# A scalar broadcast to 128 partitions by DMA at the head of the sync queue, with the first x load moved to the ACT queue

One core of a Trainium2 chip. The metric is the device time of one execution in microseconds (us).

## The reference

```python
def setup_inputs():
    B, S, D = 512, 32, 640
    # x, fx: (B, S, D) bfloat16; alpha: (1,) bfloat16

def reference(x, fx, alpha):
    return x + alpha * fx
```

Two tensors of 20.97 MB are read and one is written: 62.92 MB in all, and one multiply-add for each element.

## The kernel before

Each tensor is seen as 128 partitions by 81920 columns and cut into five chunks of 16384 columns (4.19 MB, 32 KB a partition). VectorE computes `f * alpha + x` on a chunk in place. It needs alpha as a column, one value a partition. The kernel before loads alpha as a single element and spreads it with a matmul against a row of ones.

```python
def alpha_to_lanes(nc, consts, psum, alpha, eng):
    P = nc.NUM_PARTITIONS
    a_1 = consts.tile([1, 1], alpha.dtype, name="a_1")
    eng.dma_start(out=a_1[:], in_=alpha[None, :])
    ones = consts.tile([1, P], alpha.dtype, name="ones")
    nc.vector.memset(ones[:], 1.0)
    a_ps = psum.tile([P, 1], F32, name="a_ps")
    nc.tensor.matmul(a_ps[:], ones[:], a_1[:], start=True, stop=True)
    a_f = consts.tile([P, 1], F32, name="a_f")
    nc.vector.tensor_copy(out=a_f[:], in_=a_ps[:])
    return a_f
# ... (pools: xs has 4 buffers, fs has 2)
    a_f = alpha_to_lanes(nc, consts, psum, alpha, nc.scalar)

    def load_x(k):
        xt[k] = xs.tile([P, CHUNK], x.dtype, tag="x", name="x_t")
        nc.sync.dma_start(out=xt[k][:], in_=xv[:, bass.ts(k, CHUNK)])

    def load_f(k):
        ft[k] = fs.tile([P, CHUNK], fx.dtype, tag="f", name="f_t")
        nc.sync.dma_start(out=ft[k][:], in_=fxv[:, bass.ts(k, CHUNK)])
# ...
    load_x(0)
    load_f(0)
    load_x(1)
    load_f(1)
    load_x(2)
    compute(0)
    load_f(2)
    store(0)
    load_x(3)
    compute(1)
# ... (goes on in this way; the last chunk is computed and stored in two halves)
```

All large transfers, stores too, go through the sync queue in this order. In the profile each issuing queue appears as a ring (q1 belongs to SyncE, here "sync" or SP; q10 to ScalarE, "ACT"). A ring's transfers are carried out by 16 DMA engines, and each is recorded as packets, here one for each partition's row.

Of the kernel before, what the change touches and what calls it, by code (L numbers as in the profile page):

```python
# [1 line left out]

# [4 lines left out]

ACT = mybir.ActivationFunctionType
ALU = mybir.AluOpType
F32 = mybir.dt.float32  # L10
BF16 = mybir.dt.bfloat16

CHUNK = 16384


def alpha_to_lanes(nc, consts, psum, alpha, eng):

    P = nc.NUM_PARTITIONS
    a_1 = consts.tile([1, 1], alpha.dtype, name="a_1")
    eng.dma_start(out=a_1[:], in_=alpha[None, :])  # L20
    ones = consts.tile([1, P], alpha.dtype, name="ones")
    nc.vector.memset(ones[:], 1.0)  # L22
    a_ps = psum.tile([P, 1], F32, name="a_ps")
    nc.tensor.matmul(a_ps[:], ones[:], a_1[:], start=True, stop=True)  # L24
    a_f = consts.tile([P, 1], F32, name="a_f")
    nc.vector.tensor_copy(out=a_f[:], in_=a_ps[:])  # L26
    return a_f


@with_exitstack  # L30
def kernel(
    ctx: ExitStack,
    tc: tile.TileContext,
    x: bass.AP,
    fx: bass.AP,
    alpha: bass.AP,
    out: bass.AP,
):
    nc = tc.nc
    P = nc.NUM_PARTITIONS  # L40
    xv = x.flatten_outer_dims().rearrange("(p n) d -> p (n d)", p=P)
    fxv = fx.flatten_outer_dims().rearrange("(p n) d -> p (n d)", p=P)
    ov = out.flatten_outer_dims().rearrange("(p n) d -> p (n d)", p=P)
    F = xv.shape[1]
    K = F // CHUNK
    assert K * CHUNK == F and K == 5

    consts = ctx.enter_context(tc.tile_pool(name="consts", bufs=1))
    psum = ctx.enter_context(tc.tile_pool(name="psum", bufs=1, space=bass.MemoryType.PSUM))
    xs = ctx.enter_context(tc.tile_pool(name="xs", bufs=4))  # L50
    fs = ctx.enter_context(tc.tile_pool(name="fs", bufs=2))
    ctx.enter_context(tc.manual_schedule())

    a_f = alpha_to_lanes(nc, consts, psum, alpha, nc.scalar)
    xt, ft = {}, {}

    def load_x(k):
        xt[k] = xs.tile([P, CHUNK], x.dtype, tag="x", name="x_t")
        nc.sync.dma_start(out=xt[k][:], in_=xv[:, bass.ts(k, CHUNK)])  # L59

    def load_f(k):
        ft[k] = fs.tile([P, CHUNK], fx.dtype, tag="f", name="f_t")
        nc.sync.dma_start(out=ft[k][:], in_=fxv[:, bass.ts(k, CHUNK)])

    def compute(k, parts=1):
        n = CHUNK // parts
        for j in range(parts):
            s = bass.ts(j, n)
            nc.vector.scalar_tensor_tensor(  # L69
                out=xt[k][:, s],  # L70
                in0=ft[k][:, s],
                scalar=a_f[:],
                in1=xt[k][:, s],
                op0=ALU.mult,
                op1=ALU.add,
            )

    def store(k, j=0, parts=1):
        n = CHUNK // parts
        nc.sync.dma_start(  # L80
            out=ov[:, k * CHUNK + j * n : k * CHUNK + (j + 1) * n],
            in_=xt[k][:, bass.ts(j, n)],
# [12 lines that stand above are left out]
    load_f(3)  # L95
    store(1)
    load_x(4)
    compute(2)
    load_f(4)
    store(2)  # L100
    compute(3)
    store(3)
    compute(4, 2)
    store(4, 0, 2)
    store(4, 1, 2)


# [1 line left out]
_INS = ['x', 'fx', 'alpha']  # L109
_OUTS = [((512, 32, 640), 'bfloat16')]  # L110


# [23 lines left out]
```

## Time and profile before

| | before |
|---|---|
| time, median of 3 | 152.79 us (152.72 to 152.88) |
| span of the profiled run | 150.6 us |
| sync queue's share of 16 DMA engines | 98.0% |
| VectorE busy | 86.9 us (58%) |
| bytes moved, mean rate | 62.92 MB, 418 GB/s |

How to read it: a resource that is busy for 98% of the span bounds the kernel. Work on other engines then matters only if it makes that resource start later, pause or do more. The lines behind this are in the prediction.

### The profile page before, as it was taken

How to read it: one execution, taken by the hardware profiler on the slowest of the kernel's cores; microseconds unless marked ns; L12 is line 12 of the kernel's file. 1: busy time of each engine (PE TensorE's matmuls, PEld its weight loads, DVE VectorE, ACT ScalarE, POOL GpSimd, SP SyncE). 2: the span in 40 equal slices, each digit the busy share in tenths (PEclk: the TensorE clock that was granted, in tenths of full speed). 3: DMA queues.
4: the chain of work that ended last, by engine and by line, in shares of the span. 5: the costliest groups of instructions: out<-in, count | busy, mean ns of one | idle time of the engine just before them, and what ended most of it. 6: DMA issues, size and time to landing. Idle time of an engine off the chain costs nothing.

```text
span 150.6 us, 85 instructions
## 1 busy us (share of the span) xinstructions
PE 0.2 (0%) x1; PEld 0.1 (0%) x1; DVE 86.9 (58%) x8; POOL 0.2 (0%) x4
## 2 busy tenths in 40 slices
PE   0000000000000000000000000000000000000000
PEld 0000000000000000000000000000000000000000
DVE  0000009999679998499991006999900089997000
POOL 0000000000000000000000000000000000000000
DMA  6999999999999999799999999999999999999994
GB/s 200 444 453 435 418 418 418 418 444 453 444 453 435 418 418 418 339 444 470 418 418 418 418 418 435 435 435 453 426 435 444 418 418 435 435 435 405 426 444 205
DMA packets 2306, 62.92 MB, mean 418 GB/s; under 512 B 258, under 2 KB 258, under 8 KB 258
## 3 DMA queue, kind: packets, MB, share of 16 engines
q1 hardware_dynamic: 2304, 62.92, 98.0%
q10 hardware_dynamic: 2, 0.00, 0.0%
HBM read 41.94 MB, written 20.97 MB: 418 GB/s over the span
## 4 chain that ended last, share of the span: by engine, by line
DMA 56%; DVE 29%; DVEq 6%; issue 0%; SPq 0%
DMA f_t<-in_fx_dram 56%; DVE x_t L69 29%; DVEq L131 6%; SPq L59 0%; DVEq L69 0%
## 5 line engine op out<-in xcount | busy, mean ns | idle before, releaser
L69 DVE SCALAR_TENSOR_TENSOR x_t<-f_t,a_f,x_t 128x16384 bf16<-128x16384 bf16 (+1 forms) x6 | 86.6, 14439 | 49.5 <-DMA f_t<-in_fx_dram 49.5
L26 DVE COPY a_f<-a_ps 128x1 f32<-128x1 f32 x1 | 0.2, 159 | 1.1 <-PE a_ps L24 1.1
L22 DVE MEMSET ones<- 1x128 bf16 x1 | 0.2, 165 | 0.8 <-PEq L120 0.8
L24 PE MATMUL a_ps<-a,ones 1*128 1x1 bf16 x1 | 0.2, 159 | 1.9 <-DMA a<-in_alpha_dram 1.9
L120 POOL MEMSET const-bfloat16-1.0<- 128x1 bf16 x1 | 0.1, 102 | 0.0
L120 POOL MEMSET const-uint8-127<- 128x1 uint8 x1 | 0.1, 102 | 0.0
L24 PEld LDWEIGHTS <-ones 1*128 1x128 bf16 x1 | 0.1, 100 | 1.0 <-DVE ones L22 1.0
L120 POOL MEMSET const-float32-0.0<- 128x1 f32 x1 | 0.1, 99 | 0.2 <-issue 0.2
L120 POOL MEMSET const-float32-1.0<- 128x1 f32 x1 | 0.1, 99 | 0.0
## 6 DMA issues: line engine op xcount, KB each, us to landing
x_t<-in_x_dram SPq DMA_DIRECT2D x5, 4096.0 KB, 34.8
f_t<-in_fx_dram SPq DMA_DIRECT2D x5, 4096.0 KB, 32.1
out_dram<-x_t SPq DMA_DIRECT2D x4, 4096.0 KB, 36.5
out_dram<-x_t SPq DMA_DIRECT2D x2, 2048.0 KB, 15.2
a<-in_alpha_dram ACTq DMA_DIRECT2D x1, 0.0 KB
```

What stands on the lines that cost most here:

```text
L22: nc.vector.memset(ones[:], 1.0)
L24: nc.tensor.matmul(a_ps[:], ones[:], a_1[:], start=True, stop=True)
L26: nc.vector.tensor_copy(out=a_f[:], in_=a_ps[:])
L69: nc.vector.scalar_tensor_tensor(out=xt[k][:, s], in0=ft[k][:, s], scalar=a_f[:], in1=xt[k][:, s], op0=ALU.mult, op1=ALU.add,)
L120: nc = _bacc.Bacc("TRN2", target_bir_lowering=False, num_devices=1)
L131: with _tile.TileContext(nc) as tc:
```

## The change

Its intent: alpha comes as a finished column in one DMA, so that memset, matmul and PSUM (where the matmul's result goes) are not needed, and the first x load does not queue behind it, since it is issued from another engine at the same time.

```diff
-def alpha_to_lanes(nc, consts, psum, alpha, eng):
+def alpha_to_lanes(nc, consts, alpha, eng):
     P = nc.NUM_PARTITIONS
-    a_1 = consts.tile([1, 1], alpha.dtype, name="a_1")
-    eng.dma_start(out=a_1[:], in_=alpha[None, :])
-    ones = consts.tile([1, P], alpha.dtype, name="ones")
-    nc.vector.memset(ones[:], 1.0)
-    a_ps = psum.tile([P, 1], F32, name="a_ps")
-    nc.tensor.matmul(a_ps[:], ones[:], a_1[:], start=True, stop=True)
+    a_b = consts.tile([P, 1], alpha.dtype, name="a_b")
+    eng.dma_start(out=a_b[:], in_=alpha.to_broadcast((P, 1)))
     a_f = consts.tile([P, 1], F32, name="a_f")
-    nc.vector.tensor_copy(out=a_f[:], in_=a_ps[:])
+    nc.vector.tensor_copy(out=a_f[:], in_=a_b[:])
     return a_f
# ... (the PSUM pool goes)
-    a_f = alpha_to_lanes(nc, consts, psum, alpha, nc.scalar)
+    a_f = alpha_to_lanes(nc, consts, alpha, nc.sync)
     def load_x(k):
         xt[k] = xs.tile([P, CHUNK], x.dtype, tag="x", name="x_t")
-        nc.sync.dma_start(out=xt[k][:], in_=xv[:, bass.ts(k, CHUNK)])
+        eng = nc.scalar if k == 0 else nc.sync
+        eng.dma_start(out=xt[k][:], in_=xv[:, bass.ts(k, CHUNK)])
```

More of the change, by code (lines that the diff above doesn't have):

```diff
@@ L48 @@
     consts = ctx.enter_context(tc.tile_pool(name="consts", bufs=1))
-    psum = ctx.enter_context(tc.tile_pool(name="psum", bufs=1, space=bass.MemoryType.PSUM))
     xs = ctx.enter_context(tc.tile_pool(name="xs", bufs=4))
```

## The prediction

> **What bounds the kernel now.** I read the page's summary and its DMA queue part first, to see which resource is full. Then I read the table by stretches, to see whether it is full all the time, and last the timeline and the waits of the sync queue, to see who could let it run dry.
>
> The head of the page and the queue part:
>
> ```profile
> span 150.6 us, 85 instructions
> PE 0.2 (0%) x1; PEld 0.1 (0%) x1; DVE 86.9 (58%) x8; POOL 0.2 (0%) x4
> ...
> q1 hardware_dynamic: 2304, 62.92, 98.0%
> q10 hardware_dynamic: 2, 0.00, 0.0%
> HBM read 41.94 MB, written 20.97 MB: 418 GB/s over the span
> ```
>
> The sync queue's ring (q1) keeps all 16 DMA engines busy for 98.0% of the span. VectorE has 86.9 of 150.6 us. The ACT ring (q10) carries only alpha: one datum and one semaphore write, 2 packets. So this is a copy machine with an add beside it. Bytes over rate: the table by stretches gives the steady rate.
>
> ```profile
> 5.00:30.00 25.00, 0.00 (x0) 0.00 (x0) 7.16 (x1) 0.00 (x0) 1.00 1.00 431
> 30.00:60.00 30.00, 0.00 (x0) 0.00 (x0) 27.41 (x2) 0.00 (x0) 1.00 1.03 435
> 60.00:90.00 30.00, 0.00 (x0) 0.00 (x0) 17.28 (x1) 0.00 (x0) 1.00 0.99 422
> 90.00:120.00 30.00, 0.00 (x0) 0.00 (x0) 17.29 (x1) 0.00 (x0) 1.00 0.99 429
> ```
>
> The last two columns are the DMA share and GB/s. The share is 0.99 or more in every stretch, at about 431 GB/s. 62.92 MB at 431 GB/s is 146.0 us. The span has 4.6 us more: the same table cut finely shows no bytes before some point in 1.5 to 2.0 us and none after 149.0 (of 150.6), which is about 3.2 us; the remaining 1.4 us are the fill of the first packets and small dips. A change can therefore act on the time only through the moment at which the first bytes flow, the work or pauses added to the DMA engines, or a moment at which the queue runs empty.
>
> The chain of waits blames fx loads (56%) and VectorE (29%), which is how a transfer behind others in one FIFO looks: the f_t load "takes" 21.55 us from issue to landing because x_t's 4.19 MB stand before it (2 x 4.19 MB / 431 GB/s = 19.5 us, plus the start). I do not read that chain as a bound by VectorE: the DMA engines are full while VectorE runs.
>
> The start, from the timeline:
>
> ```profile
> 0.73 0.38 SPq L59 DMA_DIRECT2D x_t<-in_x_dram  x1
> 0.73 0.49 ACTq L20 DMA_DIRECT2D a<-in_alpha_dram  x1
> ...
> 1.16 0.43 SPq L63 DMA_DIRECT2D f_t<-in_fx_dram  x1
> ...
> 2.11 0.16 DVE L26 COPY a_f<-a_ps 128x1 f32<-128x1 f32 x1 [1.13 <-PE a_ps L24]
> ...
> 22.84 17.28 DVE L69 SCALAR_TENSOR_TENSOR x_t<-f_t,a_f,x_t 128x16384 bf16<-128x16384 bf16 x1 [20.57 <-DMA f_t<-in_fx_dram]
> ```
>
> SP and ACT issue their first DMAs at the same moment, 0.73 us. The alpha column is ready at 2.11 + 0.16 = 2.27 us, and its first reader starts at 22.84: the alpha path has 20.6 us of slack now.
>
> Can the queue run dry? The sync queue's own waits:
>
> ```profile
> SPq L80 <- DVE x_t L69: 55.5, 3, 28.7
> SPq L63 <- DVE x_t L69: 41.6, 3, 17.4
> ```
>
> Large, but harmless. Five loads are issued by 3.2 us, good for 5 x 4.19 MB / 431 = 48.7 us, that is till about 50; the sixth load is issued at 40.16 us, when the first multiply-add ends. There are 10 us in hand, and the later issues, counted the same way, have 6 us (the last half store) or more.
>
> **What the Trainium skill says.** (1) "DMA: Bandwidth & Descriptors", section "Issuing engines are not separate DMA queues": DMAs from sync, scalar and gpsimd run on the same 16 engines and interleave; several issuers save only sequencer time. The trace before fits: one ring alone already fills the engines to 98.0%. (2) The same page, "Queues, rings and completion order": an engine takes turns between the rings that have work, switching at packet boundaries. Nothing in the trace before shows it, as q10 carried only 2 packets; the changed kernel will. (3) The same page, "Bandwidth", the measured table: a 4 KB load to 128 partitions has a floor of about 0.67 us, read there as about 10.5 ns a packet. It is for DMAs issued from GpSimd, and no row of this trace has a load of 128 tiny elements. (4) The same page, "Specifications": below 512 B a transfer is not at line rate, because of a read-modify-write. The 258 packets under 512 B of the trace before, spread over the run, leave the share at 0.99 or more, so small packets as such are not dear here.
>
> **The change, part by part.**
>
> *Removed:* on VectorE one memset (0.165 us), on PE a weight load and a matmul (0.10 and 0.16 us), a PSUM tile, and two hand-overs between engines. All lie before 2.27 us with 20.6 us of slack. Worth 0 us. The copy to f32 (0.16 us) stays and now reads SBUF; it still lies ahead of the first multiply-add on VectorE, which waits anyway.
>
> *Moved: the first x load to ACT.* ACT issues at 0.73 us as SP did; its one issue took 0.49 us against 0.38, so the first bytes may come some 0.1 us later, or not at all later. Cost 0 to +0.1 us. The bytes are the same, and x and fx of the first chunk now share the engines instead of following each other. The multiply-add needs both, and both together are still 8.39 MB, so the pair lands as before, about 22.7 us. No other issue changes its order.
>
> *Added: alpha as 128 elements of 2 bytes at the head of the sync ring.* One issue of about 0.4 us on SP pushes the fx issue from 1.16 to about 1.6 us. In the kernel before that would be a loss only if the engines had nothing to do; here they have 9.7 us of x from the ACT ring. So 0 us. On the engines it is 128 / 16 = 8 small packets each, plus a semaphore write each. By the page's 10.5 ns (an estimate from that table) 8 x 10.5 = 84 ns, say +0.1 us; if the whole floor of 0.67 us had to be paid with the engines idle, +0.7 us. As x runs beside it, I choose the low end.
>
> *Sum:* 0 (removed) + 0.05 (start) + 0.1 (tiny packets) = +0.15 us of span; 152.79 + 0.15 = 152.94, call it 152.9 us.
>
> **The rivals.**
>
> *A: the tiny packets hold up their ring.* If an engine takes turns strictly, each of the 8 alpha packets waits for an x packet of 32 KB (9.7 us / 8 = 1.2 us), so alpha lands only around 10 to 12 us, and x lands at about the same time, well ahead of fx. This still leaves some 10 us of slack, and engines never idle: +0 us. Only if each tiny access stalled the engine itself (its latency not hidden) would it show: at an assumed 0.3 us each, 2.4 us, thus about 155.2. Against: the semaphore packets do not stall anything visible.
>
> *B: two rings run worse or better than one.* Two read streams from different tensors in turns could cost or gain in HBM. It lasts only as long as both rings have work, at most 20 us. Five per cent of that is 1 us either way: 151.8 to 153.8. For: the slices of before already wander between 418 and 453 GB/s. Against: they do that with one ring, and reads beside writes in the middle of the run keep 435.
>
> *C: a gain from the two issuers.* Shorter alpha path, fewer engines, issue time in parallel: none is on the path, since the ring is ready before the engines need it. At most the fill of the first packets overlaps, -0.3 us: 152.5.
>
> *D: the queue runs dry.* If the first pair landed more than 10 us late, the sixth load would come too late. Nothing in the sum comes near it.
>
> **Range and chances.** The runs of before lie within 0.16 us. The range must hold a cheaper start (C, -0.3), noise between chips (some 0.3%, a guess of mine, 0.4 us) and the full floor of the alpha load (+0.7): 152.3 to 153.7. The 2% borders are at 149.7 and 155.8. Faster by 2% would need 3.1 us out of a span with only 4.6 us that is not transfer at the steady rate: 0.01. Slower by 2% needs rival A with a real stall of 0.4 us for each tiny packet: 0.03. Within 2%: 0.96.
>
> **What would show it right or wrong.** The queue part of the page: q10 should carry 128 x packets and 16 semaphore packets (144, 4.19 MB), and packets under 512 B should rise from 258 to about 400, as 128 elements and 16 semaphores replace two. In the timeline, the ACT issue stands at about 0.73 us, the fx issue near 1.6, the f32 copy waits for the alpha DMA and starts somewhere between 2.5 and 12 us, and the first multiply-add starts at 22.5 to 23.5 us. In the stretches, 5 to 30 us should show 425 to 437 GB/s and the later ones what they showed before. The chain still names fx loads. I am wrong if the stretch up to 30 us drops below 420 GB/s (B), if no bytes flow until well after 2 us (start), if the copy of alpha starts after 20 us and the first multiply-add waits for it (A), or if there is a stretch later with a share under 0.95 (D).

## More of the kernel before

All runs told here were at a granted clock of 1.0.

One more line of the page is needed later, the rate in 40 equal slices of the span (3.77 us each):

```profile
GB/s 200 444 453 435 418 418 418 418 444 453 444 453 435 418 418 418 339 444 470 418 418 418 418 418 435 435 435 453 426 435 444 418 418 435 435 435 405 426 444 205
```

Slices 3 and 4 (7.5 to 15 us) run at 453 and 435 GB/s. Slice 17 (60 to 64 us) is a dip, 339 GB/s, just before the first store.

## The result

| | before | after |
|---|---|---|
| time, median of 4 | 152.75 us (152.33 to 152.88) | 153.65 us (153.30 to 153.85) |
| ratio | | 1.0061 (1.0034 to 1.0088) |
| span of the profiled run | 150.6 us | 151.9 us |
| first multiply-add starts | 22.84 us | 24.58 us |

Here and below a ratio is the mean time of one kernel's fast runs over that of the other's in the same rounds, with a 95% interval (in the experiments without the first run of each side), so it is not quite the ratio of the medians quoted. The kernel is slower by 0.6%: clear of noise, but "same" by the border of 2%.

The changed kernel's page, its rate in 40 slices and its queue part:

```profile
GB/s 216 440 328 345 440 423 431 414 440 449 431 440 431 431 414 423 449 449 431 431 423 423 423 414 449 449 431 423 431 423 414 431 466 449 423 423 397 431 419 168
DMA packets 2448, 62.92 MB, mean 414 GB/s; under 512 B 400, under 2 KB 400, under 8 KB 400
...
q1 hardware_dynamic: 2304, 58.72, 89.9%
q10 hardware_dynamic: 144, 4.19, 7.2%
```

Slices 3 and 4 have dropped from 453 and 435 to 328 and 345 GB/s: the loss sits between 7.6 and 15 us. Slice 17 has risen from 339 to 449: some is given back at 60 us. The small packets are 400, as counted in advance.

Its start, from the timeline:

```profile
0.72 0.54 SPq L20 DMA_DIRECT2D a_b<-in_alpha_dram  x1
0.73 0.36 ACTq L55 DMA_DIRECT2D x_t<-in_x_dram  x1
1.32 0.57 SPq L59 DMA_DIRECT2D f_t<-in_fx_dram  x1
...
14.73 0.15 DVE L22 CAST a_f<-a_b 128x1 f32<-128x1 bf16 x1 [14.73 <-DMA a_b<-in_alpha_dram]
24.58 17.29 DVE L65 SCALAR_TENSOR_TENSOR x_t<-f_t,a_f,x_t 128x16384 bf16<-128x16384 bf16 x1 [9.70 <-DMA f_t<-in_fx_dram]
```

A load of 256 bytes took 14 us to land. It still came 9.7 us before its reader could start, because that waits for fx. So alpha's lateness is not the cost; what its packets do to the DMA engines is. The table by stretches, changed kernel:

```profile
5.00:30.00 25.00, 5.58 (x2) 0.00 (x0) 1.00 0.97 405
30.00:60.00 30.00, 27.90 (x2) 0.00 (x0) 1.00 1.00 434
60.00:90.00 30.00, 18.53 (x2) 0.00 (x0) 1.00 1.00 429
90.00:120.00 30.00, 17.29 (x1) 0.00 (x0) 1.00 1.00 430
```

From 5 to 30 us it moved 405 GB/s where before moved 431: 25 us x 26 GB/s = 0.65 MB, at 431 GB/s 1.5 us. These tables are coarse: a packet counts whole in the stretch in which it starts (the kernel before has a "share" of 3.23 from 1.5 to 2.0 us). The first multiply-add, which waits for the same loads, starts 1.74 us later; the expectations below, written from tables, say about 1.6 us.

What happens there can be read in the trace's records of single packets. This is one DMA engine of the changed kernel (put together by matching each packet's start to the end of the one before; times from the first large packet; q10 is ACT's ring, q1 SP's):

```
start ns   took ns  ring  bytes
   22       1694    q10   32768
 1713       1324    q10   32768
 3033       1213    q10   32768
 4243          9    q1        2
 4249       1213    q10   32768
 5458          9    q1        2
 5464       1213    q10   32768
 6673          9    q1        2
 6679       1472    q10   32768
 8150          7    q1        2
 8153       1524    q10   32768
 9662          9    q1        2
 9667       1408    q10   32768
```

The rings take turns one for one: a row of x (32 KB), an element of alpha (2 bytes). The small packet itself is on record with 7 to 9 ns. But from the third turn on the x row beside it takes 1.4 to 1.5 us in place of 1.213, and when x is through, the last alpha elements leave the engine idle. I summed both over all engines from the packet records, in the 25 us from the first packet of either ring: idle time of 16 engines, and time of 32 KB packets above 1.213 us, each divided by 16. Before: 0.29 + 0.74 = 1.03 us (the fill of the first packets). Changed: 1.08 + 1.33 = 2.41 us. So the early loss is 1.4 us. Around the first store (50 to 65 us) the large packets lengthen, or stretch, by 0.87 us before and by 0.02 us after: 0.85 us given back. The engines finish less evenly: idle time in the last 12 us is 0.41 and 0.94 us, 0.5 us lost. 1.4 - 0.85 + 0.5 is about 1.1 us of the 1.3 us between the two spans. That last term isn't clear of chance: it compares one profile with one, and in e6 below, which lost nothing early, the same idle time is about 0.8 us.

### The profile page after: what moved, and what is told of

Same layout as the page of the kernel before. It is cut to its first block, busy times and chain, and to the rows that moved or that the text cites. A ratio compares the mean times of both kernels' runs of the same rounds, so it can differ in the third digit from the quotient of the medians.

```text
span 151.9 us, 81 instructions
## 1 busy us (share of the span) xinstructions
DVE 86.7 (57%) x7; POOL 0.2 (0%) x4
## 2 busy tenths in 40 slices
DMA packets 2448, 62.92 MB, mean 414 GB/s; under 512 B 400, under 2 KB 400, under 8 KB 400
## 4 chain that ended last, share of the span: by engine, by line
DMA 57%; DVE 29%; DVEq 6%; SPq 0%; issue 0%
DMA f_t<-in_fx_dram 57%; DVE x_t L65 29%; DVEq L127 6%; SPq L20 0%; DVEq L65 0%
## 5 line engine op out<-in xcount | busy, mean ns | idle before, releaser
L22 DVE CAST a_f<-a_b 128x1 f32<-128x1 bf16 x1 | 0.2, 153 | 14.7 <-DMA a_b<-in_alpha_dram 14.7
```

What stands on the lines that cost most here:

```text
L22: nc.vector.tensor_copy(out=a_f[:], in_=a_b[:])
```

## The experiments

Twelve kernels, each timed in 5 rounds beside the kernel before. The batches ran on different chips: e1 to e4 on chip 11, e5 to e8 on chip 8, e9 to e11 on chip 10, e12 on chip 13. "By 30 us" is the mass moved in the first 30 us of the profiled run, from the table by stretches (5 us x the rate of the first stretch + 25 us x that of the second); it includes a late start. "Stretch at 60 us" is no stretch of the table but a lengthening: the sum described above of the time of 32 KB packets over 1.213 us, from 50 to 65 us.

| kernel | median us | before, same rounds | ratio | 95% interval | by 30 us, MB | stretch at 60 us |
|---|---|---|---|---|---|---|
| before (its own profile) | | | | | 12.06 | 0.87 |
| changed | 153.65 | 152.75 | 1.0061 | 1.0034 to 1.0088 | 11.47 | 0.02 |
| e1 move alone | 152.80 | 152.62 | 0.9999 | 0.9965 to 1.0034 | 12.06 | 0.98 |
| e2 broadcast alone | 153.60 | 152.62 | 1.0057 | 1.0021 to 1.0092 | 11.55 | 0.69 |
| e3 broadcast behind first fx | 153.65 | 152.62 | 1.0071 | 1.0026 to 1.0117 | 11.38 | 0.00 |
| e4 broadcast twice | 154.06 | 152.62 | 1.0090 | 1.0055 to 1.0125 | 11.01 | 0.05 |
| e5 128 places | 152.71 | 152.77 | 1.0022 | 0.9988 to 1.0056 | 12.07 | 0.65 |
| e6 128 rows of 512 B | 152.95 | 152.77 | 1.0015 | 0.9988 to 1.0043 | 12.13 | 0.74 |
| e7 broadcast to 64 | 153.17 | 152.77 | 1.0035 | 1.0000 to 1.0069 | 12.05 | 1.02 |
| e8 late issue alone | 152.99 | 152.77 | 1.0020 | 0.9998 to 1.0042 | 12.05 | 0.93 |
| e9 128 neighbours | 153.54 | 152.68 | 1.0055 | 1.0032 to 1.0079 | 11.49 | 0.04 |
| e10 broadcast as a probe | 153.69 | 152.68 | 1.0074 | 1.0042 to 1.0106 | 11.51 | 0.04 |
| e11 one row of 512 B, 128 times | 154.97 | 152.68 | 1.0154 | 1.0128 to 1.0181 | 11.54 | 0.04 |
| e12 late by plain bytes | 155.25 | 152.63 | 1.0138 | 1.0091 to 1.0186 | 12.18 | 0.84 |

The start of the first multiply-add checks the column "by 30 us" without its coarseness. It is 22.84 us before; 22.89 in e1, 22.95 in e5, 23.05 in e7, 23.07 in e6, 23.14 in e8; and 24.20 in e2, 24.46 in e10, 24.47 in e9, 24.58 in the changed kernel, 24.72 in e3, 25.04 in e11, 25.41 in e4 (24.75 in e12, which moves 0.72 MB more first).

The theory after the result (S): the small packets of alpha cost. Its rivals: two rings at work together cost (R); only the taking of turns does (A); the late issue does; and, later, that it is not their size but the place they read (H).

### First batch: which part of the change

**e1_move_alone**: the x load moves, alpha stays as it was (one element, matmul) but heads the sync queue.

```diff
 # against the kernel before
-    a_f = alpha_to_lanes(nc, consts, psum, alpha, nc.scalar)
+    a_f = alpha_to_lanes(nc, consts, psum, alpha, nc.sync)
-        nc.sync.dma_start(out=xt[k][:], in_=xv[:, bass.ts(k, CHUNK)])
+        eng = nc.scalar if k == 0 else nc.sync
+        eng.dma_start(out=xt[k][:], in_=xv[:, bass.ts(k, CHUNK)])
```

> The move alone: the first x load on the ACT queue, alpha as before as one element (with memset and matmul), now heading the sync queue. Profile of the changed kernel: between 5 and 20 us after its start it moved 389 and 381 GB/s where the kernel before moved 417 and 459, so about 1.6 us went there; in that time alpha's small packets take turns one for one with x's packets of 32 KB. Theory S (the small packets cost, about 0.2 us for each of the 8 on an engine): this kernel has one small packet in all, so 152.7 us +-0.2, same as before, and 5 to 20 us shows at least 430 GB/s; x and fx share the rings. Theory R (two rings with work in turns cost by themselves): at least as slow as the changed kernel, 153.6 us or more, since both rings now hold large packets for 20 us.

Measured: 0.9999, and 12.06 MB by 30 us, as before. x and fx now share the engines through two rings for 20 us. Its stretch from 5 to 30 us:

```profile
5.00:30.00 25.00, 0.00 (x0) 0.00 (x0) 7.11 (x1) 0.00 (x0) 1.00 1.00 431
```

Two rings of large packets cost nothing that shows. Theory R falls.

**e2_bcast_alone**: the broadcast stays, x goes back to the sync queue, behind it.

```diff
 # against the changed kernel
-        eng = nc.scalar if k == 0 else nc.sync
+        eng = nc.sync
```

> The broadcast alone: alpha to 128 partitions heads the sync queue, the first x load stays behind it in the same queue. Theory S (a small packet costs wherever it stands): +1.0 to +1.6 us, so 153.7 to 154.3, with alpha landing before 4 us and the first x bytes later by that much. Theory A (only the taking of turns between two rings costs, since a large packet is not fetched ahead across the turn): +0 to +0.3 us, 152.7 to 153.0. Theory R: +0.

Measured: 1.0057, with one ring only. So taking turns is not needed for the cost, and theory A falls in its strict form. The time, 153.6, is just under theory S's range. But here x is also issued later (1.32 us), so part of it could be the late start; e8 measures that.

**e3_bcast_behind_f0**: the changed kernel with the broadcast behind the first fx load.

```diff
 # against the changed kernel
-    a_f = alpha_to_lanes(nc, consts, alpha, nc.sync)
 # ...
     load_x(0)
     load_f(0)
+    a_f = alpha_to_lanes(nc, consts, alpha, nc.sync)
```

> The first x load on ACT, the broadcast of alpha in the sync queue behind the first fx load. x and fx (8 packets of 32 KB each on an engine) take turns; alpha's 8 small packets then come when x is through or nearly so, in one ring. Theory S: the same loss as in the changed kernel, +0.9 us, merely later, around 20 us. Theory A: no turns with small packets, so less than +0.4 us. Theory R: +0.9 or more from the turns of x and fx.

Measured: 1.0071, the same loss as in the changed kernel, now near 20 us: the stretch from 20 to 30 us moved 351 GB/s (before: 419). Theory S's time and place are right. A new cost joins it: the first multiply-add now waits for alpha (its copy ran at 24.53 us).

**e4_bcast_twice**: the changed kernel with a second broadcast into an unused tile.

```diff
 # against the changed kernel
     eng.dma_start(out=a_b[:], in_=alpha.to_broadcast((P, 1)))
+    a_c = consts.tile([P, 1], alpha.dtype, name="a_c")
+    eng.dma_start(out=a_c[:], in_=alpha.to_broadcast((P, 1)))
```

> The changed kernel with a second, unused broadcast of alpha behind the first: 16 small packets an engine ahead of fx in place of 8, of which the last 8 or more have no x packet left to alternate with. Theory S: the loss doubles, so +0.9 us more than the changed kernel (about 154.5), up to +1.6 us more if each of the added ones costs 0.2 us (155.2). Theory A: the added ones have no partner and cost little: within 0.3 us of the changed kernel, 153.6 to 153.9. Theory R: same as the changed kernel.

Measured: 154.06, 0.4 us above the changed kernel's 153.65 of other rounds; S had asked for 0.9 at least, A for 0.3 at most. By 30 us it is 1.05 MB behind the kernel before (2.4 us), the changed kernel 0.59 MB (1.4 us). More packets cost more, but not twice.

### Second batch: what of the small packets costs

These keep the first x load on ACT and alpha as one element the old way, as e1 does (which cost nothing), and put a load into an unused tile ahead of everything on the sync queue. Results stay correct; only the head of the queue differs.

```diff
 # against e1
+    probe = consts.tile([P, 1], x.dtype, name="probe")
+    nc.sync.dma_start(out=probe[:], in_=...)
     a_f = alpha_to_lanes(nc, consts, psum, alpha, nc.sync)
 # e5:  tile [P, 1],   in_=xv[:, 0:1]                        128 places, 160 KiB apart, 2 bytes each
 # e6:  tile [P, 256], in_=xv[:, 0:256]                      128 places, 512 bytes each
 # e7:  tile [64, 1],  in_=alpha.to_broadcast((64, 1))       one word, 64 times
 # e9:  tile [P, 1],   in_=xv[0:1, 0:P].rearrange("o p -> p o")   128 neighbours within 256 bytes
 # e10: tile [P, 1],   in_=alpha.to_broadcast((P, 1))        one word, 128 times
 # e11: tile [P, 256], in_=xv[0:1, 0:256].to_broadcast((P, 256))  one row of 512 bytes, 128 times
 # e12: tile [P, 2816], in_=xv[:, 0:2816]                    128 places, 5632 bytes each
```

**e5_distinct**

> The small packets without alpha's common address: the first x load on ACT; the sync queue is headed by a load into an unused tile of 128 elements of 2 bytes at 128 different places (column 0 of x), then alpha as one element (old way), then fx. Known so far: the move alone costs nothing (152.8 against 152.62 us), each kernel with the broadcast costs 0.9 us or more. Theory D (any small packet costs its own latency because nothing large runs on that engine meanwhile): like the changed kernel, about +0.9 us, 153.4 to 153.8, and 5 to 20 us moves 380 to 400 GB/s. Theory H (128 reads of the same word of memory get in each other's way): like the move alone, within 0.2 us of before.

Measured: median 152.71 against 152.77 us, and no loss in the window: 12.07 MB by 30 us. It has as many 2-byte packets (402 under 512 B; the changed kernel 400), but they run earlier: by the packet records from 0.07 us before the first large packet to 6.6 us after it, half of them by 0.3 us, where the changed kernel's run from 4.1 to 12.7 us. The fair partner is therefore e9, whose small packets run from -0.3 to 7.7 us. Two of its six runs were at 153.8, so the ratio's interval reaches 1.0056; it is the window that decides. The rate in slices, e5:

```profile
GB/s 192 427 462 444 418 427 418 418 427 436 453 462 436 427 427 418 366 436 436 436 418 418 427 409 470 436 444 427 436 436 418 418 418 444 453 436 388 427 440 200
```

Slices 3 and 4 are whole: 462 and 444 GB/s, and the packet records show no lengthened large packet and no idle time from 3 us after the first large packet to 25 us, a time in which a quarter of the small packets still run. Theory D falls.

**e6_rows_512B**

> As e5_distinct, but each of the 128 packets is a row of 512 bytes instead of 2 (64 KB in all, 0.15 us at 431 GB/s). Theory W (packets below 512 bytes cost because their target must be read, changed and written): no more than +0.2 us. Theory D (a small packet costs its latency whatever its size): like e5_distinct plus 0.15, so about +1.0 us. Theory H: +0.15 us.

Measured: 1.0015, 12.13 MB by 30 us, no loss. As e5 with 2 bytes had lost nothing either, the limit of 512 bytes, from the page that the prediction cites, is not what costs. Theory H's +0.15 us fits, but so would zero (interval 0.9988 to 1.0043).

**e7_bcast_64**

> Half the dose: the first x load on ACT, the sync queue headed by a broadcast of alpha to 64 partitions (an unused tile; 4 small packets on an engine), then alpha as one element the old way. In the changed kernel the window of the small packets lost about 1.6 us and the time 0.9. If the cost is proportional to the number of small packets: window loss 0.8 us, time +0.4 to +0.5 us. If the first few are free, having been fetched ahead behind the first x packets (in the changed kernel, x packets stretch only from the third small packet on): within 0.2 us of before.

Measured: 1.0035, with single times from 152.54 to 154.44 us, so the time alone doesn't decide. By 30 us it had moved 12.05 MB, as before: no loss that this table shows with 4 packets an engine, where 8 lose 1.4 us and 16 lose 2.4. The packet records are finer: from 6 to 12 us after the first large packet e7 loses 0.17 us (0.15 of lengthened large packets, 0.02 idle), e10 1.28 us (0.49 and 0.79), and e5, e6 and e8, on e7's own chip, 0.00. So the cost isn't proportional: the first few cost little, not nothing. Where the rest of e7's 0.4 us of median comes from stays open.

**e8_issue_only**

```diff
 # against the kernel before
-    a_f = alpha_to_lanes(nc, consts, psum, alpha, nc.scalar)
+    a_f = alpha_to_lanes(nc, consts, psum, alpha, nc.sync)
```

> What the late issue of x alone costs in e2_bcast_alone (there x was issued at 1.32 us instead of 0.73): kernel before with alpha as one element at the head of the sync queue instead of the ACT queue, everything else the same, one packet. Alpha's issue takes about 0.34 us there, so x is issued at about 1.12 us. If the start of the first bytes sets the time one for one: +0.4 us, 153.0; and then 0.6 us of e2's 0.9 are its late issue. If it is hidden: same as before.

Measured: 1.0020 (0.9998 to 1.0042), half of the 0.4 us, and not clear of zero. It moved 12.05 MB by 30 us where e2 moved 11.55. So the late issue explains at most a part of e2; most of e2's 0.9 us is the broadcast. (e2 issues x another 0.2 us later than e8, which the difference includes.)

### Third batch: the same place

**e9_neighbours**

> As e5_distinct, but the 128 elements of 2 bytes are the first 128 of x, next to each other within 256 bytes of memory, rather than 160 KiB apart. Theory H1 (reads of one small piece of memory by all 16 engines queue up there, not only reads of the very same word): like the broadcast, 5 to 20 us loses about 1.6 us and the time is +0.9. Theory H2 (only a repeated address costs): like e5_distinct, no loss.

Measured: 1.0055, 11.49 MB by 30 us. The 128 addresses are all different, and yet the loss is that of the broadcast; e5's kernel differs from it by nothing but the distance between the addresses, though it ran on another chip. So it isn't the repeated address or the zero step that costs: it is that the engines read one small piece of memory. H1 holds, H2 falls. A difference between the chips is a rival that no run excludes, as no kernel with far-apart small packets ran on chip 10 and no full broadcast on chip 8. Against it: the broadcast costs alike on chips 11 and 10 (e3, e10), and on chip 8 itself 64 reads of one word lengthened large packets (e7, 0.15 us) where 128 reads of different places lengthened none. The table by stretches of e5 (first fence) and e9 (second):

```profile
0.00:5.00 5.00, 0.00 (x0) 0.10 (x1) 0.17 (x1) 0.20 (x4) 1.00 0.70 243
5.00:12.00 7.00, 0.16 (x1) 0.00 (x0) 0.16 (x1) 0.00 (x0) 1.00 0.99 426
```

```profile
0.00:5.00 5.00, 0.00 (x0) 0.10 (x1) 0.17 (x1) 0.20 (x4) 1.00 0.62 203
5.00:12.00 7.00, 0.16 (x1) 0.00 (x0) 0.16 (x1) 0.00 (x0) 1.00 0.93 379
```

The loss comes earlier than with alpha: from the first microseconds on, 203 in place of 243 GB/s.

**e10_bcast_probe**

> Control for the probe kernels: the full broadcast of alpha to 128 partitions into an unused tile at the head of the sync queue, alpha for use as one element the old way behind it, the first x load on ACT. If the cost comes from the 128 reads of one word, this behaves as the changed kernel: about +0.9 us, 380 to 390 GB/s from 5 to 20 us. If the cost came from anything else in the changed kernel (the copy from a bf16 column, the missing matmul path), it is as before.

Measured: 1.0074, 11.51 MB by 30 us, and the dent is the changed kernel's own. Its rate in slices:

```profile
GB/s 197 454 326 352 446 420 412 420 454 446 454 420 412 412 446 454 429 446 420 403 429 446 446 429 437 420 412 420 454 454 446 403 412 420 429 463 390 429 437 64
```

326 and 352 in slices 3 and 4 (changed kernel: 328 and 345), while memset and matmul are still there. From 5 to 20 us it moved 395 GB/s, a little above the 380 to 390 expected. So the probes are a fair stand-in, and the path of alpha on VectorE and PE plays no part.

**e11_same_row_512B**

> As e6_rows_512B, but all 128 packets read the same row of 512 bytes (a broadcast of 256 elements of x). Theory H (reads of one place queue up): like the broadcast of alpha or dearer, +0.9 us or more, while e6 with 128 different rows lost nothing in the window. If only repeated elements of 2 bytes are bad: within 0.3 us of before.

Measured: 154.97 us, 1.0154, the dearest of the probes, where e6 with as many bytes from 128 rows was at 1.0015. The first multiply-add of e6 (first fence) and of e11 (second):

```profile
23.07 17.29 DVE L72 SCALAR_TENSOR_TENSOR x_t<-f_t,a_f,x_t 128x16384 bf16<-128x16384 bf16 x1 [11.19 <-DMA f_t<-in_fx_dram]
```

```profile
25.04 17.29 DVE L72 SCALAR_TENSOR_TENSOR x_t<-f_t,a_f,x_t 128x16384 bf16<-128x16384 bf16 x1 [11.97 <-DMA f_t<-in_fx_dram]
```

Packets of 512 bytes are not spared, so the place decides and not the size (again across two chips, 8 and 10). By 30 us its loss (11.54 MB) is no greater than that of the broadcast. The profile also has an uneven end, 1.70 us of idle engine time in the last 12 us against 0.41 before; but e10's profile, taken in its slowest run (154.68 us), has about 1.6 us too. Why e11 costs more than e10 stays open.

**e12_late_by_bytes**

> Why the changed kernel keeps 0.9 of the about 1.6 us that its small packets lose. In the profile of before (and of six probes) the x-and-fx packets stretch by 0.6 to 1.0 us in all around 56 to 60 us, ahead of the first store; in the changed kernel and five others, all late by 1.5 us or more in their first multiply-add, that stretch is 0.03 us or less. Here the first x load is on ACT and the sync queue is headed by a plain load of 128 different rows of 5632 bytes (0.72 MB, 1.67 us at 431 GB/s) into an unused tile: late by as much, with no two packets reading one place. If lateness alone takes the later stretch away: stretch under 0.1 us and time about +0.8 us. If the stretch is tied to something else that the queueing reads change: stretch 0.6 to 1.0 us stays and time +1.5 to +1.8 us.

Measured: the stretch at 60 us stayed (0.84 us), and the time rose by 1.0138, about 2.1 us by the mean of the runs, a little more than the 1.5 to 1.8 us expected (2.6 us by the medians). Its 12.18 MB by 30 us include the probe's 0.72 MB; of x and fx it had moved about 11.46. So lateness as such does not remove that stretch. The dip just before the first store, in the kernel before (first fence), the changed kernel (second) and e12 (third), from the table by stretches:

```profile
60.00:62.00 2.00, 0.00 (x0) 0.00 (x0) 0.00 (x0) 0.00 (x0) 1.00 0.72 295
```

```profile
60.00:62.00 2.00, 1.25 (x1) 0.00 (x0) 1.00 0.88 377
```

```profile
62.00:64.00 2.00, 0.00 (x0) 0.00 (x0) 0.00 (x0) 0.00 (x0) 1.00 0.61 262
```

e12 has its dip 2 us later, as it is 2 us late. These fences are coarse: e11, whose packets hardly lengthen (0.04 us), has 0.72 and 311 GB/s from 60 to 62 us as well, so it is the sum over packets that decides. By that sum the lengthening is missing in the six kernels whose one-place reads cost clearly while large transfers were under way (changed, e3, e4, e9, e10, e11), and there in the eight others: e7 with its 0.17 us among them, and e2, which has the same reads with nothing beside them. What those reads leave behind 40 us later was not found. Each kernel has one profile, so the count is six against eight and no more.

No experiment beat the kernel before: it moves 62.92 MB with its DMA engines 98% busy, and e1 and e5 only equal it.

## Why the prediction was right or wrong

The time was right, if only just: 153.65 us lies 0.05 us within the range's upper end, the change is within 2% as given 0.96, and its direction was foreseen. The point, 152.9, was 0.75 us low: it forecast +0.15 us, and +0.9 was measured, six times as much. Of its signs, the packet counts, the two issues at 0.73 us and the later stretches came true; alpha's copy (14.73 us, said to start by 12), the first multiply-add (24.58 us, said to start by 23.5) and the early stretch (405 GB/s, said to be 425 to 437) did not.

- **The bound.** Right. With DMA as the bound, dropping memset, matmul and PSUM gained nothing, and nothing before 20 us on other engines mattered. Alpha landed 12 us later than before, with no effect.
- **Removed, 0 us.** Right: e10, which keeps the matmul path, has the changed kernel's time (153.69 us).
- **Moved, 0 to +0.1 us.** Right: e1 measures 0.9999. ACT's issue took 0.36 us, even less than in the kernel before. The fx issue was said to move from 1.16 to about 1.6 us, which overlooked that the x issue leaves SP when alpha's comes: it stood at 1.32.
- **Added, +0.1 us.** This is the step that failed. The working took 8 packets at 10.5 ns each and chose the low end "as x runs beside it". The early loss was 1.4 us (2.41 - 1.03), or 0.17 us for each of an engine's 8 packets. Large packets beside the small ones did not hide it: they lengthened, and engines stood idle. The conclusion that small packets are not dear held for those from far-apart places (e5: no loss), but it was the wrong property. Its evidence, the semaphore packets of the kernel before, could not show it: where they read is in no view. Alpha's 128 all read one place, and e5 against e9 and e6 against e11 point to that as what costs. The 10.5 ns, too, is the floor of a whole load divided by 64 packets in the table that the prediction cites, which doesn't call it one engine's cost for a packet.
- **Sum.** Two further terms were not foreseen at all: 0.85 us given back at 60 us, and about 0.5 us lost to engines that finish unevenly. That the net of +0.9 us still fell within the range is luck: without the 0.85 us given back the time would have been about 154.5 (an estimate, 153.65 + 0.85). The range reached to 153.7 only by an allowance for the floor of 0.67 us, a different cost.
- **Rival A** came nearest: turns one for one, seen packet by packet, and it named a condition under which they cost ("each tiny access stalled the engine itself"). It then set that aside, and said that the engines never idle (1.08 us of idle time measured). That the place read matters it didn't see. Its assumed 0.3 us each was nearer to the 0.17 us measured than the sum was. Its place for alpha's landing, 10 to 12 us, was a little early (14.7).
- **Rival B** had set the sign "below 420 GB/s up to 30 us". The sign appeared (405), yet two rings are not the cause. A sign that two causes share tells nothing apart; e1 was needed.
- **Rivals C and D**: no gain from two issuers, and the queue never ran dry.

What stays open: how small "one place" must be (256 and 512 bytes cost, 160 KiB apart does not); whether it takes 16 engines at one place, or one engine's 8 reads of it would do; by what mechanism such reads cost (that they queue up is a name for it, as no view shows a queue); whether e5 and e9 would differ as much on one chip; why the first four packets of an engine cost little; and why the stretch before the first store vanishes.

## What to carry to other kernels

In a kernel bound by DMA, look at a new small load not for its bytes but for what it makes 16 engines do: a load that sent all of them to one spot of memory took the place of more than a microsecond of large transfers here (1.4 us), while the same number of tiny packets from places far apart cost nothing that showed (e5). A scalar that is needed on all partitions was better fetched once and spread on an idle engine, as the kernel before did, with slack for it (20.6 us here). And when a dent in the rate appears where predicted, test the cause separately: several explain it.

## What the Trainium skill lacked or had wrong

- "DMA: Bandwidth & Descriptors", "Rules for kernel authors", allows a repeated source ("A source may repeat (a broadcast)") and names no price. Here 128 packets that read one word cost 0.6% to 0.7% (changed kernel, e10), 128 that read within 256 bytes 0.55% (e9), 128 that read one row of 512 bytes 1.5% (e11), while different rows or elements 160 KiB apart lost nothing in the window (e5, e6).
- The same page, "Bandwidth": about 10.5 ns a packet, its floor of 0.67 us divided by 64 packets. It doesn't say whether these are the whole load's or one engine's, nor that the place read matters. With one place read by all, 8 packets an engine lost 1.4 us: 170 ns for each of an engine's packets, or 11 ns for each of the load's 128; from far-apart places (e5) no loss showed.
- The same page, "Specifications": below 512 B not at line rate. It lacks what this means beside other traffic: 128 elements of 2 bytes from 128 places left the first 30 us at 12.07 MB (before: 12.06).
- The same page, "Queues, rings and completion order": turns at packet boundaries, a packet being typically 9 to 17 descriptors. The turns are there, but here a turn, as the trace records it, is a single row of 32 KB against a single element of 2 bytes.
- No page has the stretch of large packets ahead of the first store (0.65 to 1.02 us in all in eight of fourteen profiles).
